# An attention-then-soft-MoE kernel: V's beacons loaded into a tile of their own, slot inputs with x as the stationary operand, and a reordered output group

## The chip, the cores and the metric

The kernel runs on one core of a Trainium2 chip. The core has a matrix engine (TensorE, PE in the profile, whose weight loads are listed as PEld), a vector engine (VectorE, DVE), a scalar engine (ScalarE, ACT), a general engine (GpSimd, POOL) and a sync engine (SP), and its transfers run on 16 DMA engines. In this kernel SP issues the loads of q, k, v and the beacons and the stores of the output (queue q1 of the profile), and POOL issues the loads of the expert weights, which are turned from float32 into float16 on the way (queue q0). The metric is the device time of one execution in microseconds (us); lower is better. The profile comes from one execution, and the times from several.

## The reference

Attention with 16 beacon keys and values ahead of the 576 causal ones, per batch and head, and behind it a soft mixture of experts over all 4608 tokens:

```python
B, H, S, Nb, D = 8, 8, 576, 16, 64
k_all = concat([beacon_k, k], axis=2); v_all = concat([beacon_v, v], axis=2)
scores = q @ k_all.T / sqrt(D)           # causal mask on the 576 keys, none on the beacons
a = softmax(scores); attn = a @ v_all
x = attn.transpose(0, 2, 1, 3).reshape(4608, 512)
logits = x @ phi                         # 32 slots: 8 experts of 4
slot_input = softmax(logits, axis=0).T @ x
slot_out[e] = relu(slot_input[e] @ w1[e]) @ w2[e]     # w1 512x1024, w2 1024x512
out = softmax(logits, axis=1) @ slot_out
```

## The kernel before

The order of all instructions is written out by hand. The main loop runs over 32 pairs of heads (`n`, four to a batch), and `lists[n]` names the pieces of work of one pass in order: `S0` to `S3` are the four score steps (PE into PSUM, then an exponential on ACT into the tile `ex`, then causal masks by POOL on the steps 1 to 3; `M` is the mask of step 0, on DVE). `A0` and `A1` multiply the previous pair's `ex` by V and, after `A1`, DVE normalises into `xb` (L434 and L435). `Qa`, `Qb`, `Ka` and `Kb` transpose q and k of later pairs on PE and copy them out on DVE (L377). `X0`, `X12` and `X34` transpose x, `L0` and `L1` make the logits of a half batch, `D` transposes the exponentials into `dT`, and `SI` adds one batch to the slot inputs.

V reaches the core as float32 in the tiles `vr` (two loads per batch, 128 partitions, two rows of V per partition, three buffers) and `vl` (the last rows), and POOL converts it into the float16 tile `vh` of the batch: pieces `c0`, `c1` (`cast_r`, L441, one 128x1024 instruction each) and `e0`, `e1` (`cast_vl`, L457, two 48x256 instructions each). `d0` and `d1` (`dup`, L451, DVE) copy a part of `vh` into `vd`. The first of the two `vr` loads of a batch (L145) brings 128 partitions, of which the first 8 are the place of the beacons; `load_bv` (L152) then loads the batch's beacons over these 8 partitions, so it waits until the first load has landed. `c0` converts both together. Loads are asked for one or two passes ahead through the table `asks`; SP issues them in that order, each when its buffer is free.

`SI` has two forms. For batches 0 to 5 it is `si_moving` (L564): `dT` is the stationary operand, 32 columns wide, and x moves, 512 columns at a time, in five matmuls; DVE adds the 128x512 result to `siq` (L568). `si_turn` (piece `SX`, L574, once, in pass 30) sums the four groups of rows of `siq` and turns them into `siacc` with eight float32 matmuls against the constant `slc`. For batches 6 and 7 it is `si_piece` (L551): x is the stationary operand (a 128x128 weight load for each of 20 matmuls) and `dT` moves, 32 columns, and DVE adds a 128x128 result (L556).

The expert weights come in 37 tiles of 2048 float16 columns. `want(n)` sets how many POOL has issued by pass `n`; the last ones (`wx`) go into the buffers of q and k that have become free and are loaded in halves. The very last six (L209) hold the left halves (`hf` 0) and then the right halves (`hf` 1) of the last three tiles of w2. POOL clears `hTz` (L696) ahead of the last seven issues.

After the loop come the last logits, layer 1 (L764), `turn` (L781) and layer 2 (L794) of the experts. `slot_out(0)` ends the left 256 columns of the slot outputs `soh` and `slot_out(1)` the right ones, which need the last weights. `group(cg, o, w)` makes the output of 512 tokens for `w` columns from column `o`: four matmuls (L838), each read out of PSUM by ACT (L840) or DVE (L843) in turn, and a store for every two. The order is: groups 0 and 1 left, `slot_out(1)`, group 2 left, groups 0 to 2 right, then groups 3 to 8 whole.

Of the kernel before, what the change touches and what calls it, by code (L numbers as in the profile page):

```python
# [8 lines left out]
FP = mybir.dt.float32  # L9
F16 = mybir.dt.float16  # L10
BF = mybir.dt.bfloat16
AL = mybir.AluOpType
# [5 lines left out]
def kernel(  # L18
# [21 lines left out]
    NCH = 5  # L40
    UL = U - 4 * P
    UE = (UL + Nb) // 2
    J = S // 64
    NP = B * H // 2
    NDC = Dm // P
# [31 lines left out]
    POS = [0, 2, 1, 3, 4]  # L77
# [50 lines left out]
    vr, vl = {}, {}  # L128
    vrows = v.rearrange("b h s d -> (b h s) d")

    def load_r(b, r):
# [15 lines left out]
        else:  # L147
            nc.sync.dma_start(out=t[:, :, :], in_=v[b, :, 2 * P - Nb:4 * P - Nb, :].rearrange(
                "h (p t) d -> p h (t d)", t=2))

    def load_bv(b):
        nc.sync.dma_start(out=vr[(b, 0)][0:Nb // 2],  # L152
                          in_=beacon_v[b].rearrange("h (p t) d -> p h (t d)", t=2))


    bv0 = exq.tile([P, H, 2 * D], FP, name="bv0", tag="ex")
# [72 lines left out]
    def dcols(x, c):  # L229
        o = 2 * P * (c // 2) + c % 2  # L230
        return x[:, o:o + 2 * P - 1:2]
# [70 lines left out]
    siT = const.tile([P, NDC, NSL], F16, name="siT")  # L302


    siq = const.tile([P, Dm], FP, name="siq")
    slc = const.tile([P, NSL], FP, name="slc")
# [8 lines left out]
    scs = [ps_sc.tile([P, 2, 512], FP, name=f"sc{i}") for i in range(2)]  # L315

    def late_constants():
        nc.vector.memset(siq[:, :], 0.0)
        nc.gpsimd.memset(slc[:, :], 0.0)
        for c in range(P // NSL):  # L320
            nc.gpsimd.affine_select(out=slc[:, :], in_=slc[:, :], compare_op=AL.not_equal, fill=1.0,
                                    base=-NSL * c, pattern=[[-1, NSL]], channel_multiplier=1)
        nc.gpsimd.memset(ssel[:, :, :], 0.0)
        for gr in range(E // EG):
            for i in range(EG):
                nc.gpsimd.affine_select(
                    out=ssel[:, gr, i * SPE:(i + 1) * SPE], in_=ssel[:, gr, i * SPE:(i + 1) * SPE],
                    compare_op=AL.not_equal, fill=1.0,
                    base=-(NSL * i + (gr * EG + i) * SPE), pattern=[[-1, SPE]], channel_multiplier=1)
# [115 lines left out]
    def cast_bv0():  # L445
        nc.vector.tensor_copy(
            out=vh[0][0:Nb // 2, 0:2, :, 0:D].rearrange("p s h d -> p h s d"),
            in_=bv0[0:Nb // 2].rearrange("p h (s d) -> p h s d", s=2))

    def dup(b, r):  # L450
        nc.vector.tensor_copy(out=vd[b % 2][64 * r:64 * r + 64, :, r, :, :],  # L451
                              in_=vh[b % 2][0:64, 2 * r:2 * r + 2, :, :])

    def cast_vl(b, r):
        t = vl[b]
        for i in range(2):
# [103 lines left out]
    def si_moving(b):  # L560
        sp = ps_tr.tile([P, Dm], FP, name="tr", tag="tr")
        for i in range(NCH):
            m, c = P if i < 4 else UL, i % 4
            nc.tensor.matmul(  # L564
                sp[NSL * c:NSL * c + NSL, :], dT[b][0:m, i, :],
                xb[b % 2][0:m, POS[i], :, :].rearrange("p h d -> p (h d)"),
                start=i < 4, stop=i in (1, 2, 3, 4))
        nc.vector.scalar_tensor_tensor(out=siq[:, :], in0=sp[:, :], scalar=2.0 ** -8,  # L568
                                       in1=siq[:, :], op0=AL.mult, op1=AL.add)

    def si_turn():
        sp = ps_tr.tile([P, NDC, NSL], FP, name="tr", tag="tr")
        for t in range(NDC):
            nc.tensor.matmul(sp[:, t, :], dcols(siq, t), slc[:, :],  # L574
                             start=True, stop=True)
        nc.vector.tensor_copy(out=siacc[:, :, :], in_=sp[:, :, :])

    order = ["S1 A0 L1 M S2 Qa Qb S3 A1 Ka S0", "S1 D A0 SI M S2 Kb S3 A1 X0 c0 S0",
             "S1 A0 M S2 Qa Qb S3 A1 X12 d0 c1 S0", "S1 A0 L0 M S2 e0 Ka Kb S3 A1 X34 d1 e1 S0"]
    lists = {n: order[n % 4].split() for n in range(NP)}


    lists[0] = "S2 M bv S3 S0 c1 d0 d1 e0 e1".split()
    lists[1] = "S1 S2 S3 M T2 A0 A1 S0".split()
    lists[2] = "S1 A0 M BC S2 T3 A1 S3 S0 BT c0".split()  # L590
    lists[3] = "S1 A0 M S2 T4 e0 A1 S3 e1 T5 c1 S0".split()
    lists[4] = "S1 A0 M d0 S2 Qa Qb S3 A1 d1 Ka S0".split()
    lists[5] = "S1 A0 M S2 Kb S3 A1 X0 c0 S0".split()
    lists[NP - 5] = "S1 A0 L0 M S2 Ka Kb S3 A1 X34 e0 S0".split()
    lists[NP - 4] = "S1 A0 L1 M S2 Ta Tb S3 e1 A1 d1 S0".split()
    lists[NP - 3] = "S1 D A0 SI M S2 Ta Tb S3 A1 X0 S0".split()
    lists[NP - 2] = "S1 A0 X12 M S2 X34 A1 L0 S3 SX S0".split()
    lists[NP - 1] = "S1 A0 P0 M S2 P1 A1 L1 S3 D".split()
    routing = {"X0": lambda b: xt_piece(b, (0,)), "X12": lambda b: xt_piece(b, (1, 2)),
               "X34": lambda b: xt_piece(b, (3, 4)), "L0": lambda b: logit_piece(b, 0),  # L600
               "L1": lambda b: logit_piece(b, 1), "D": lambda b: dt_piece(b),
               "SI": lambda b: (si_moving if b < B - 2 else si_piece)(b)}


    def idle_work(t, m):
# [3 lines left out]
    def do(n, w):  # L609
        b, g = divmod(n, H // 2)  # L610
        if w in routing:
            rb = b - 1
            if w == "SI" or n < NP - 1 and w in ("L1", "D"):
                rb = b - 2
            if rb >= 0:
                routing[w](rb)
        elif w in ("Qa", "Qb", "Ka", "Kb"):
            transp4(n // 2 + 1, "QK".index(w[0]), "ab".index(w[1]))
        elif w[0] == "T":
            m, ws = (n + 2, ("ab".index(w[1]),)) if w[1] in "ab" else (int(w[1]), (0, 1))  # L620
            for x in ws:
                transp(m, x)
        elif w == "BC":
            beacon_cast(1, B)
        elif w == "BT":
            beacon_t(1, B)
        elif w == "M":
            mask_f(n)
        elif w == "SX":
            si_turn()  # L630
        elif w[0] == "P":
            xt_pair(int(w[1]))
        elif w[0] == "A":
            if n >= 1:
                attend(n - 1, int(w[1]))
        elif w == "S0":
            if n + 1 < NP:
                score(n + 1, 0)
        elif w[0] == "S":
            score(n, int(w[1]))  # L640
        elif w == "bv":
            cast_bv0()
        elif w[0] in "cde":

            vb = 0 if n < 2 else b if g == 0 else b + 1
            if vb >= B:
                pass
            elif w[0] == "e":
                cast_vl(vb, int(w[1]))
            elif w[0] == "c":  # L650
# [33 lines left out]
    for n in range(NP):  # L684
        b, g = divmod(n, H // 2)
        if n + 2 < NP and n not in (2, 3):
            beacon_k_in(n + 2, nc.gpsimd)
        for w in lists[n]:
            if n == 3 and w == "M":
                beacon_k_in(n + 1, nc.gpsimd)  # L690
                beacon_k_in(n + 2, nc.gpsimd)
            if n == 6 and w == "M":
                for r in range(4):
                    nc.vector.tensor_copy(out=phih[:, :, r, :], in_=phif[:, :, :])
            if n == NP - 1 and w == "D":
                nc.gpsimd.memset(hTz, 0.0)  # L696
            if w == ("e0" if n == 3 else "D" if n == NP - 1 else "S0"):
                while wl < want(n):
                    load_w(wl)
                    wl += 1  # L700
            do(n, w)
        for what, vb in asks.get((n, 0), []):
            what(vb)
        for m in (5, 6) if n == 0 else (n + 6,):
            if m < NP:
                load_pair(m)
        for what, vb in asks.get((n, 1), []):
            what(vb)
# [119 lines left out]
    sc_scope.close()  # L828
    ps_f = ctx.enter_context(tc.tile_pool(name="ps_f", bufs=4, space=PSUM, side="right"))

    def group(cg, o, w):
        dst = out[cg * P * G:(cg + 1) * P * G, :].rearrange("(p j) d -> p j d", j=G)
        for j0 in range(0, G, 2):
# [58 lines left out]
```

## Time and profile before

| | us |
|---|---|
| median of 3 runs | 196.21 (194.69, 196.21, 201.97) |
| the profiled execution's own time | 195.3 |
| its span, first to last instruction | 193.6 |
| busy in the span: PE / DVE / ACT / POOL | 156.8 / 146.6 / 129.5 / 119.1 |
| period of the loop per batch (xb at 57.73, 75.00 and 92.25) | 17.27 and 17.25 |
| last weight issue at, landing after | 158.4, 10.3 |
| issue of output stores, from and to | 166.5, 187.8 |

Times inside the profile count from the start of the span. A row such as "POOL ex L387 <- ACT ex L403: 32.8, 49, 1.9" reads: the instruction at line 387 on POOL waited in total 32.8 us, 49 times, at most 1.9, for line 403 on ACT. Rates of transfers count the bytes that are written: a weight that is read as float32 and written as float16 counts half of what is read from memory. In the tables of stretches each engine has its busy time with the number of instructions; the last three columns are the granted TensorE clock, the busy share of the 16 DMA engines (packets of two queues may overlap, so it can be over 1) and GB/s.

### The profile page before, as it was taken

Reading aid. Unit: us, or ns where it says so; the run is one execution under the profiler, and the core shown is the slowest. Engines: PE = TensorE matmul, PEld = TensorE weight load, DVE = VectorE, ACT = ScalarE, POOL = GpSimd, SP = SyncE. Lnnn points to the kernel's source line nnn. Section 1 sums busy time; section 2 is a strip of 40 time slices with the busy share of each in tenths; the row PEclk is TensorE's granted clock in tenths of the full one; section 3 lists DMA queues with packets and bytes.
Section 4 is the critical chain, followed back from the end, with each engine's and each line's share of the span. In section 5 each row is a group of like instructions: output and inputs, shape, how many; then the busy total and the mean of one; then the engine's idle time right before and its main releaser. Section 6 shows DMA issues by size and latency. Waiting matters only on the chain.

```text
span 193.6 us, 7169 instructions
## 1 busy us (share of the span) xinstructions
PE 156.8 (81%) x2985; PEld 110.3 (57%) x2985; DVE 146.6 (76%) x306; ACT 129.5 (67%) x190; POOL 119.1 (62%) x278
## 2 busy tenths in 40 slices
PE   2569996989998989999998999999889999688300
PEld 1327674666676756767665766677567867343000
DVE  3595999989898988889898987997776524599500
ACT  3474876878788878879877877888668131399400
POOL 7996597678478858856875888697756860000000
PEclk9999999999999999999999999999999999999855
DMA  5999999999999999999999999999999999999995
GB/s 182 324 334 367 374 349 294 290 325 242 282 275 346 285 260 314 312 305 263 370 287 271 299 295 311 259 261 225 215 216 212 210 203 197 198 362 407 419 420 232
DMA packets 45048, 56.11 MB, mean 290 GB/s; under 512 B 4191, under 2 KB 30295, under 8 KB 45015
## 3 DMA queue, kind: packets, MB, share of 16 engines
q1 hardware_dynamic: 36359, 38.87, 58.7%
q0 software_dynamic: 8656, 16.78, 46.5%
q8 instruction: 23, 0.38, 0.7%
q14 instruction: 10, 0.08, 0.1%
HBM read 62.98 MB, written 9.44 MB: 374 GB/s over the span
## 4 chain that ended last, share of the span: by engine, by line
DVE 48%; PE 26%; issue 6%; DMA 5%; POOL 4%; ACT 3%; DVEq 0%; POOLq 0%; ACTq 0%
DVE xb L435 12%; PE av L426 9%; DVE qT L377 9%; DVE kT L377 8%; DMA wx<-in_moe_w_dram 5%; PE sc L396 4%; PE tr L375 4%; PE tr L486 4%; DVE ex L413 3%; DVE osb L843 3%; DVE kT L362 2%; DVE siq L568 2%; DVE qT L362 2%; ACT ex L403 2%; PE tr L564 2%
## 5 line engine op out<-in xcount | busy, mean ns | idle before, releaser
L403 ACT ACTIVATE ex<-sc 128x928 f16<-128x928 f32 (+2 forms) x128 | 106.4, 868 | 28.0 <-PE sc L396 20.6
L387 POOL TENSOR_SCALAR_AFFINE_SELECT ex<-ex 128x256 f16<-128x256 f16 x128 | 51.3, 414 | 35.4 <-ACT ex L403 32.8
L426 PEld LDWEIGHTS <-ex 128*128 128x128 f16 (+1 forms) x960 | 42.2, 106 | 18.2 <-issue 17.5
L396 PE MATMUL sc<-qT,kT 64*64 64x128 bf16 (+3 forms) x640 | 46.1, 264 | 4.8 <-DVE kT L382 2.2
L426 PE MATMUL av<-vh,ex 128*128 128x65 f16 x819 | 42.1, 199 | 0.1
L396 PEld LDWEIGHTS <-kT 64*64 64x64 bf16 (+1 forms) x640 | 17.6, 104 | 20.9 <-issue 7.9
L426 PE MATMUL av<-vd,ex 128*128 128x130 f16 x126 | 21.9, 225 | 8.7 <-DVE xb L435 6.6
L435 DVE TENSOR_TENSOR xb<-av,r 128x640 f16<-128x640 f32 (+1 forms) x32 | 26.0, 814 | 1.1
L377 DVE COPY kT<-tr 128x640 bf16<-128x640 bf16 (+1 forms) x24 | 18.0, 772 | 4.0 <-PE tr L375 4.0
L377 DVE COPY qT<-tr 128x640 bf16<-128x640 bf16 (+1 forms) x24 | 17.5, 769 | 3.2 <-PE tr L375 3.2
L413 DVE TENSOR_TENSOR ex<-ex,fmask 128x672 f16<-128x672 f16 x32 | 19.1, 595 | 0.4 <-ACT ex L403 0.2
L840 ACT ACTIVATE osb<-fp,rc 128x256 f32<-128x256 f32 (+1 forms) x24 | 12.9, 579 | 7.3 <-PE fp L838 6.7
L441 POOL CAST vh<-vr 128x1024 f16<-128x1024 f32 x15 | 16.0, 1066 | 0.1
L843 DVE TENSOR_SCALAR osb<-fp,rc 128x256 f32<-128x256 f32 (+1 forms) x24 | 13.7, 614 | 0.7 <-PE fp L838 0.6
L457 POOL CAST vh<-vl 48x256 f16<-48x256 f32 x32 | 13.2, 413 | 1.3
L838 PE MATMUL fp<-soh,eLh 128*128 128x256 f16 (+1 forms) x48 | 11.4, 325 | 2.6 <-ACT osb L840 1.5
L476 DVE COPY xT<-tr 128x512 f16<-128x512 f16 (+1 forms) x21 | 10.6, 504 | 0.9 <-PE tr L471 0.9
L471 PE MATMUL tr<-idh,xb 128*128 128x128 f16 (+1 forms) x140 | 10.8, 215 | 0.4 <-DVE qT L377 0.4
L375 PE MATMUL tr<-idb,kf 128*64 128x128 bf16 x216 | 9.9, 224 | 0.8 <-DVE qT L377 0.8
L838 PEld LDWEIGHTS <-eLh 128*128 128x128 f16 x48 | 5.3, 114 | 8.3 <-issue 6.5
L486 PE MATMUL tr<-xT,phih 128*128 128x288 f16 x56 | 9.2, 286 | 0.0
L375 PEld LDWEIGHTS <-kf 128*64 128x64 bf16 x216 | 7.1, 109 | 3.5 <-issue 3.3
(122 smaller groups left out, 199.3 us busy)
## 6 DMA issues: line engine op xcount, KB each, us to landing
w<-in_moe_w_dram POOLq DMA_DIRECT2D x27, 512.0 KB, 8.8
qf<-in_q_dram SPq DMA_DIRECT2D x32, 288.0 KB, 7.4
kf<-in_k_dram SPq DMA_DIRECT2D x32, 288.0 KB, 6.2
vr<-in_v_dram SPq DMA_DIRECT2D x15, 512.0 KB, 6.6
out_dram<-osb SPq DMA_DIRECT2D x12, 512.0 KB, 5.7
out_dram<-osb SPq DMA_DIRECT2D x11, 256.0 KB, 3.0
wx<-in_moe_w_dram POOLq DMA_DIRECT2D x10, 256.0 KB, 9.8
vl<-in_v_dram SPq DMA_DIRECT2D x16, 96.0 KB, 10.2
```

The lines of the kernel that those rows point to most:

```text
L375: nc.tensor.transpose(tp[64 * r:64 * r + 64, j - j0, :], ts[r][:, j, :].bitcast(BF)[:, 1::2], idb[:, :])
L377: nc.vector.tensor_copy(out=dst[:, :, Nb:Nb + S].rearrange("p a (s j) -> p a s j", j=J)[:, :, :, j0:j1], in_=tp[:, :, :].rearrange("p j (a ...
L387: nc.gpsimd.affine_select(out=x, in_=x, compare_op=AL.is_ge, fill=0.0, base=base, pattern=pattern, channel_multiplier=cm)
L396: nc.tensor.matmul(sc[p0:p0 + kn, a, col:col + un], kT[n // 2 % 2][64 * a:64 * a + 64, n % 2, k0:k0 + ks * (kn - 1) + 1:ks], qT[n // 2 % 2 ...
L403: nc.scalar.activation(x[:, :, o:o + w], sc[:, :, 0:w], AF.Exp, scale=scale)
L413: nc.vector.tensor_tensor(out=x, in0=x, in1=fmask[:, :].unsqueeze(1).broadcast_to([P, 2, XT + UL]), op=AL.min)
L426: nc.tensor.matmul(dst, ex[n][0:kn, a, o:o + m], rhs, start=j in first, stop=j in final)
L435: nc.vector.tensor_tensor(out=xb[b % 2][:, :, h0:h0 + dh * (na - 1) + 1:dh, :].rearrange("p i a d -> p a i d"), in0=avv[:, :, :, 0:D], in1 ...
L441: eng.tensor_copy(out=vh[b % 2][:, 2 * r:2 * r + 2, :, 0:D].rearrange("p s h d -> p h s d"), in_=vr.pop((b, r))[:, :, :].rearrange("p h (s ...
L486: nc.tensor.matmul(lp[:, 0:w], phih[:, t, :, :].rearrange("p r e -> p (r e)"), xT[b][:, t, Nb + hf * w:Nb + (hf + 1) * w], start=(t == 0), ...
L838: nc.tensor.matmul(fp_[:, 0:w], etok(cg, j), soh[:, o:o + w], start=True, stop=True)
L843: nc.vector.tensor_scalar(out=osb[:, j - j0, o:o + w], in0=fp_[:, 0:w], scalar1=rc[:, i:i + 1], scalar2=None, op0=AL.mult)
```

## The change

V's beacons of the batches 1 to 7 get a tile `bv` of their own (one buffer, 64 partitions, the heads in two halves), loaded by two DMAs, and two POOL instructions per batch convert them into the first 8 partitions of `vh` after `c0` has written there (pieces `b0` and `b1`). For the last batch the load is asked for half a pass later. `siq`, `slc`, `si_moving` and `si_turn` go; every batch uses `si_piece`, and `siacc` is cleared by POOL at the start. In the lists of passes 2 to 5 some of the pieces `c0`, `d0`, `d1`, `e0` and `e1` move. `hTz` is cleared as float32, with half as many elements. `slot_out(1)` moves from ahead of group 2 left to between its two halves.

```diff
     def load_bv(b):
-        nc.sync.dma_start(out=vr[(b, 0)][0:Nb // 2],
-                          in_=beacon_v[b].rearrange("h (p t) d -> p h (t d)", t=2))
+        bvs[b] = vlp.tile([64, H // 2, 2 * D], FP, name="bv", tag="bv")
+        for r in range(2):
+            nc.sync.dma_start(
+                out=bvs[b][32 * r:32 * r + Nb // 2],
+                in_=beacon_v[b, H // 2 * r:H // 2 * (r + 1)].rearrange(
+                    "h (p t) d -> p h (t d)", t=2))
...
     def late_constants():
-        nc.vector.memset(siq[:, :], 0.0)
-        nc.gpsimd.memset(slc[:, :], 0.0)
-        for c in range(P // NSL):
-            nc.gpsimd.affine_select(out=slc[:, :], in_=slc[:, :], compare_op=AL.not_equal, fill=1.0,
-                                    base=-NSL * c, pattern=[[-1, NSL]], channel_multiplier=1)
+        nc.gpsimd.memset(siacc[:, :, :], 0.0)
...
+    def cast_bv(b, r):
+        nc.gpsimd.tensor_copy(
+            out=vh[b % 2][0:Nb // 2, 0:2, H // 2 * r:H // 2 * (r + 1), 0:D].rearrange(
+                "p s h d -> p h s d"),
+            in_=bvs[b][32 * r:32 * r + Nb // 2].rearrange("p h (s d) -> p h s d", s=2))
...
-    order = ["S1 A0 L1 M S2 Qa Qb S3 A1 Ka S0", "S1 D A0 SI M S2 Kb S3 A1 X0 c0 S0",
-             "S1 A0 M S2 Qa Qb S3 A1 X12 d0 c1 S0", "S1 A0 L0 M S2 e0 Ka Kb S3 A1 X34 d1 e1 S0"]
+    order = ["S1 A0 L1 M S2 Qa Qb S3 A1 Ka S0", "S1 D A0 SI M S2 Kb S3 A1 X0 c0 b0 S0",
+             "S1 A0 M S2 b1 Qa Qb S3 A1 X12 d0 c1 S0", "S1 A0 L0 M S2 e0 Ka Kb S3 A1 X34 d1 e1 S0"]
...
-    lists[2] = "S1 A0 M BC S2 T3 A1 S3 S0 BT c0".split()
-    lists[3] = "S1 A0 M S2 T4 e0 A1 S3 e1 T5 c1 S0".split()
-    lists[4] = "S1 A0 M d0 S2 Qa Qb S3 A1 d1 Ka S0".split()
-    lists[5] = "S1 A0 M S2 Kb S3 A1 X0 c0 S0".split()
+    lists[2] = "S1 A0 M BC S2 c0 T3 A1 S3 S0 BT".split()
+    lists[3] = "S1 A0 M S2 b0 T4 A1 S3 e0 T5 c1 S0".split()
+    lists[4] = "S1 A0 M S2 b1 Qa Qb S3 A1 d0 d1 e1 Ka S0".split()
+    lists[5] = "S1 A0 M S2 Kb S3 A1 X0 c0 b0 S0".split()
...
-    lists[NP - 2] = "S1 A0 X12 M S2 X34 A1 L0 S3 SX S0".split()
+    lists[NP - 2] = "S1 A0 X12 M S2 X34 A1 L0 S3 S0".split()
...
-               "SI": lambda b: (si_moving if b < B - 2 else si_piece)(b)}
+               "SI": lambda b: si_piece(b)}
...
-        for key, what in (((n0, 0), lambda x: load_r(x, 0)), ((n1, 1), load_bv),
+        for key, what in (((n0, 0), lambda x: load_r(x, 0)),
+                          ((NP - 9, 0) if vb == B - 1 else (n1, 1), load_bv),
...
-                nc.gpsimd.memset(hTz, 0.0)
+                nc.gpsimd.memset(hTz.bitcast(FP), 0.0)
...
-    def group(cg, o, w):
+    def group(cg, o, w, js=range(0, G, 2)):
...
     for cg in range(NL):
+        group(cg, 0, HD, (0,))
         if cg == NL - 1:
             slot_out(1)
-        group(cg, 0, HD)
+        group(cg, 0, HD, (2,))
```

More of the change, by code (lines that the diff above doesn't have):

```diff
@@ L149, in load_r @@
                 "h (p t) d -> p h (t d)", t=2))
+    bvs = {}
     def load_bv(b):
-        nc.sync.dma_start(out=vr[(b, 0)][0:Nb // 2],
-                          in_=beacon_v[b].rearrange("h (p t) d -> p h (t d)", t=2))
+        bvs[b] = vlp.tile([64, H // 2, 2 * D], FP, name="bv", tag="bv")
[4 more added lines that the diff above has]
+                    "h (p t) d -> p h (t d)", t=2))
     bv0 = exq.tile([P, H, 2 * D], FP, name="bv0", tag="ex")
@@ L302 @@
     siT = const.tile([P, NDC, NSL], F16, name="siT")
-    siq = const.tile([P, Dm], FP, name="siq")
-    slc = const.tile([P, NSL], FP, name="slc")
     ssel = const.tile([P, E // EG, EG * SPE], F16, name="ssel")
@@ L558, in si_piece @@
             scalar=2.0 ** -8, in1=siacc[:, :, :], op0=AL.mult, op1=AL.add)
[L560 to L576, printed above, removed]
-    order = ["S1 A0 L1 M S2 Qa Qb S3 A1 Ka S0", "S1 D A0 SI M S2 Kb S3 A1 X0 c0 S0",
-             "S1 A0 M S2 Qa Qb S3 A1 X12 d0 c1 S0", "S1 A0 L0 M S2 e0 Ka Kb S3 A1 X34 d1 e1 S0"]
+    order = ["S1 A0 L1 M S2 Qa Qb S3 A1 Ka S0", "S1 D A0 SI M S2 Kb S3 A1 X0 c0 b0 S0",
+             "S1 A0 M S2 b1 Qa Qb S3 A1 X12 d0 c1 S0", "S1 A0 L0 M S2 e0 Ka Kb S3 A1 X34 d1 e1 S0"]
     lists = {n: order[n % 4].split() for n in range(NP)}
@@ L628, in do @@
             mask_f(n)
-        elif w == "SX":
-            si_turn()
         elif w[0] == "P":
@@ L642, in do @@
             cast_bv0()
-        elif w[0] in "cde":
+        elif w[0] in "bcde":
             vb = 0 if n < 2 else b if g == 0 else b + 1
@@ L649, in do @@
                 cast_vl(vb, int(w[1]))
+            elif w[0] == "b":
+                cast_bv(vb, int(w[1]))
             elif w[0] == "c":
@@ L829 @@
     ps_f = ctx.enter_context(tc.tile_pool(name="ps_f", bufs=4, space=PSUM, side="right"))
-    def group(cg, o, w):
+    def group(cg, o, w, js=range(0, G, 2)):
         dst = out[cg * P * G:(cg + 1) * P * G, :].rearrange("(p j) d -> p j d", j=G)
-        for j0 in range(0, G, 2):
+        for j0 in js:
             osb = wh.tile([P, 2, Dm], FP, name="osb", tag="w")
```

## The prediction

> **What bounds the kernel now.** The page first, for the transfers:
>
> ```profile
> GB/s 182 324 334 367 374 349 294 290 325 242 282 275 346 285 260 314 312 305 263 370 287 271 299 295 311 259 261 225 215 216 212 210 203 197 198 362 407 419 420 232
> HBM read 62.98 MB, written 9.44 MB: 374 GB/s over the span
> ```
>
> The rate is counted on the written side, and the weights (16.78 MB written by q0) are read as twice as much. So the 215 GB/s of the slices from about 131 to 165 us, where only weights are under way, are some 430 GB/s of reading, the 420 at the end are plain stores, and the whole is 72.4 MB in 193.6 us. The table of stretches:
>
> ```profile
> core 0: us, PE busy (x) PEld busy (x) DVE busy (x) ACT busy (x) POOL busy (x), PEclk, DMA share, GB/s
> 75.00:92.25 17.25, 15.96 (x314) 11.40 (x318) 15.00 (x30) 14.11 (x20) 12.54 (x30) 1.00 1.08 305
> ...
> 130.00:150.00 20.00, 18.02 (x359) 13.30 (x357) 15.14 (x34) 14.98 (x24) 13.52 (x32) 1.00 1.08 218
> ...
> 166.00:168.00 2.00, 1.41 (x18) 0.73 (x17) 1.75 (x4) 1.66 (x4) 0.00 (x0) 1.00 0.73 149
> 168.00:171.00 3.00, 1.86 (x13) 1.13 (x13) 1.79 (x5) 1.72 (x4) 0.00 (x0) 1.00 0.89 306
> 171.00:176.00 5.00, 4.24 (x19) 1.96 (x18) 4.91 (x9) 4.80 (x10) 0.00 (x0) 1.00 1.09 382
> 176.00:191.00 15.00, 4.21 (x15) 1.42 (x13) 5.67 (x9) 4.76 (x8) 0.00 (x0) 0.72 1.03 420
> ```
>
> The DMA engines are busy all through; the one hole is 166 to 171. In a batch of the loop (second row) three weight tiles add 1.57 MB of reading that is not counted: 305 is really 305 + 1570/17.25 = 396 GB/s. So the loop is paced by the engines, with the transfers close behind; from 130 on the transfers have a queue (the last weight takes 10.3 us to land) and set the end. Next the chain of waits:
>
> ```profile
> 51.27 0.62 PE tr L564 x5
> 51.91 0.69 DVE siq L568
> ...
> 145.21 1.07 PE tr L574 x8
> ...
> 158.40 10.28 DMA wx<-in_moe_w_dram
> ...
> 169.65 0.94 ACT osb L840 x2
> ```
>
> The slot inputs stand on the chain in the loop and at 145, but the chain then goes through the last weight (158.40 + 10.28 = 168.7). The last evacuation ends at 181, ten us before the last store lands. The left half of the last weights lands at 155.04 + 9.5 = 164.5, and PE uses it from 164.42 on: engines and transfers reach that point together. Being earlier there on the engines' side gains nothing, since the weights cannot come sooner out of a full queue; being later pushes the stores.
>
> **The change, part by part.**
>
> Beacons on SP's queue. Removed is this wait, 6.3 us in six places:
>
> ```profile
> SPq L152 <- DMA vr<-in_v_dram: 6.3, 6, 2.4
> ```
>
> Behind it on SP stand a `vr` load and the next pairs' q and k. Nobody waits for those: the only wait of PE for q is 3.8 us at the start. So 0; for the same reason the second beacon issue (0.29 us, seven times) costs 0 while q and k arrive early. Bound: if that cover were gone, 0.29 per batch, 2.0 in all.
>
> The two conversions on POOL. No row has 8x512. By free size it lies between 48x256 (0.40 us) and 128x1024 (1.07); in between, 0.63. Per batch:
>
> ```profile
> 55.84 1.31 POOL L387 TENSOR_SCALAR_AFFINE_SELECT ex<-ex 128x256 f16<-128x256 f16 x3
> 57.67 0.41 POOL L387 TENSOR_SCALAR_AFFINE_SELECT ex<-ex 128x256 f16<-128x256 f16 x1 [0.52 <-ACT ex L403]
> 58.03 1.06 POOL L441 CAST vh<-vr 128x1024 f16<-128x1024 f32 x1
> ...
> 58.60 0.22 PE L426 MATMUL av<-vd,ex 128*128 128x130 f16 x1 [0.32 <-DVE xb L435]
> ```
>
> (The first three are POOL's timeline, the last PE's.) `b0` goes ahead of the three masks, `b1` ahead of the fourth. That mask is needed by the A0 at 58.60, by its third product. POOL was idle 0.52 before it and it was ready 0.52 early, so it delays A0 by 2 x 0.63 - 1.04 = 0.22 per batch, six batches: +1.3. Bounds: 0 (at 0.40) and 6 x (2.14 - 1.04) = +6.6. Behind it `c1` runs 0.74 later, beside DVE's `vd` copy at 59.07: that row takes 0.41, but 1.28 at 29.21 beside a cast (28.96 to 30.21). The extra 0.87 falls into DVE's idle 0.70 before 60.60 and the 0.22 by which PE is late anyway: 0.
>
> A rule speaks here: the Trainium skill, SBUF — State Buffer, SBUF: two separate sides, says that VectorE in a two-port mode and GpSimd lock their shared port for a whole instruction and the other fully blocks. The row at 29.21 agrees; by the rule alone every such meeting would cost up to a whole cast, an estimate of 6 x 1.07 = 6.4 us over the loop before any cover.
>
> Slot inputs with x stationary. DVE: 0.69 becomes 0.28 (row L556), six times. PE: five matmuls (0.61) against
>
> ```profile
> 152.37 0.66 PE L551 MATMUL tr<-dT,xb 128*128 128x32 f16 x20
> 152.88 0.41 PE L512 MATMUL sc<-vh,phih 128*128 128x288 f16 x2
> ```
>
> twenty in 0.66, with the next step 0.51 after their start: equal. Of DVE's 0.41 little arrives: PE goes on without a gap from the slot input to A1's end at 53.48 and the reciprocal starts at 53.56, so at most 0.08 a batch, and I take 0.04: -0.2 (bounds 0 and -2.5). `si_turn` goes from PE's path: -1.1 at 145.
>
> The same skill's page TensorE: Matmul & The Clock Gate, Back-to-back issue gap, has pairs of weight load and matmul at 81 ns each; twenty would be an estimated 1.6 us, 1.1 more per batch. The row's 0.51/20 = 26 ns says otherwise here, and decides.
>
> At the start POOL loses 1.06 + 0.12 for `slc` and gains a memset of some 0.2; DVE loses 0.48 (`siq`). The masks and casts of the first pair follow: between 0 and -1.0, I take -0.5. The moved pieces of passes 2 to 5 are the same instructions; the one `vd` copy of 1.28 may shrink or another may grow, ±0.9, taken as 0.
>
> On the engines' side this is +1.3 - 0.2 - 1.1 - 0.5 = -0.5 at 164.4: no delay, and no gain, because the weights land at 164.5.
>
> `hTz`: 1.83 becomes about 1.08 (row 128x1040 float32) ahead of seven weight issues. 0: their landings follow each other at 0.6 to 1.5 us out of the queue, and the last issue even waits for a landing.
>
> Group 2 left. Two tiles (0.47 on ACT, 0.48 on DVE) move into the wait for the last weight: ACT is idle 1.6 us before 169.28, DVE 1.26 before 169.06. PE's two matmuls come before sixteen that end at 168.99, of which the last four wait for 168.7. So 256 KB of stores start while the engines of the hole have room: 0.26 MB / 382 GB/s = 0.69, or one evacuation of 0.48 less later; I take -0.6. The whole hole holds 2 x (382 - 149) + 3 x (382 - 306) = 0.69 MB, 1.8 us, the most that could be filled; the least is 0.
>
> **Sum.** 195.3 - 0.6 = 194.7 in the profiled execution's terms. The median shown is 0.9 above that execution, and scaled to it the sum is 195.6; with one of its three runs at 201.97 I take 195.0. About 2% is what a measurement of this kernel can tell from no change: 192.3 and 200.1 around the median.
>
> **Rivals.**
>
> *Nothing arrives* (0.14): the two tiles' stores only take the room of the last weight pieces, since these share the DMA engines. 195.3. For: at 166 to 168 weights are still landing. Against: the share there is 0.73.
>
> *The engines set the end* (0.13): if weights would come earlier with an earlier loop, every cut counts: -2.5 (`siq`), -1.1, -1.0, -0.75 (`hTz`), -0.6: 195.3 - 5.95 = 189.3. For: DVE has 48% of the chain and `siq` is on it. Against: 396 of some 425 GB/s are in use in the loop already, and the queue from 130 on.
>
> *POOL becomes late* (0.17): at 1.07 a cast, as the 128x1024 row has, A0 waits 1.1 us a batch, +6.6 - 0.2 - 1.1 - 0.5 = +4.8 at 164.4. Then the weights are all there, the DMA engines stand idle until the first store, and the reordered group hides nothing: 195.3 + 4.7 = 200.0. It starts to cost where 6 x (2c - 1.04) passes the 1.8 gained elsewhere, at 0.67 us a cast, and passes 2% (+4.0) from about 1.0. A beacon that lands late would do the same, as `b0` waits for it with all masks behind. For: four masks, three casts and a weight issue stand in one line there. Against: the row of 48x256, and POOL's 35.4 us of idle time before masks.
>
> *Weight loads of the slot inputs show* (0.04): if the 96 ns loads of L551 did not hide, 20 x 0.096 = 1.9 instead of 0.54 a batch, +8.3 - 0.5: some 203. The skill's 81 ns would give +6.0 by the same sum, an estimate. Against both: the row of L551.
>
> **How the numbers follow.** My forecast has 0.52, with its own range of 193.4 (hole filled whole, 193.5) to 196.2. Within 2%: 0.52 + 0.14 = 0.66. Faster: 0.13. Slower: 0.17 + 0.04 = 0.21. The range leaves out the engines' case and the weight loads (0.17) and takes in POOL's: 193.0 to 200.0.
>
> **What would show it.** Right: period per batch within 0.3 of 17.25; `b0` and `b1` near 0.6 us; no PE or POOL wait for beacons; last weight landing within 1 us of 168.7; the rate at 168 to 171 nearer 382; ACT at work before that landing. Wrong: a period over 18, A0 waiting for POOL masks (more than 0.3 each), or a weight landing several us earlier, which would mean that the queue was not full.

## The result: slower, and two passes of the loop that became long

The changed kernel takes 208.58 us (median of six runs, 203.5 to 209.21) against 196.28 for the kernel before (six runs, 194.69 to 201.97). The ratio is 1.044, 95% interval 1.0328 to 1.0553. The profiled execution took 203.5 us with a span of 201.8 (before: 195.3 and 193.6). The prediction was 195.0, range 193.0 to 200.0. Some runs of every kernel lie a few per cent above its others: ratios leave them out, medians do not.

The page of the changed kernel, for the transfers (granted clock and rate in 40 slices, then the queues):

```profile
PEclk9999998899999999999589999996999999999955
...
GB/s 194 281 309 353 347 296 296 288 312 293 250 282 308 264 276 309 296 238 304 322 287 277 269 327 269 250 266 228 216 214 210 207 184 194 141 316 374 408 407 263
...
q1 hardware_dynamic: 36415, 38.87, 60.5%
q0 software_dynamic: 8656, 16.78, 44.3%
...
HBM read 62.98 MB, written 9.44 MB: 359 GB/s over the span
```

The line of q1 on the page of the kernel before:

```profile
q1 hardware_dynamic: 36359, 38.87, 58.7%
```

The same 38.87 MB on q1 now takes each DMA engine 60.5% of 201.8 = 122.1 us in place of 58.7% of 193.6 = 113.6. The output stores at the end, which wait for nothing but themselves, run at 407 to 408 GB/s in place of 419 to 420. So the packets have become slower, also those of tiles that the change does not mention.

The table of stretches (us; busy PE, PEld, DVE, ACT, POOL; granted clock, DMA share, GB/s):

```profile
core 0: us, PE busy (x) PEld busy (x) DVE busy (x) ACT busy (x) POOL busy (x), PEclk, DMA share, GB/s
57.78:74.95 17.17, 15.98 (x329) 11.92 (x333) 15.28 (x30) 14.10 (x20) 13.10 (x31) 1.00 1.09 281
92.70:101.82 9.12, 6.34 (x77) 4.26 (x78) 3.94 (x7) 3.87 (x6) 7.31 (x16) 0.64 1.09 321
106.27:123.44 17.17, 15.99 (x331) 11.93 (x333) 15.29 (x31) 14.10 (x20) 13.56 (x31) 1.00 1.08 287
131.68:139.03 7.35, 5.32 (x78) 3.79 (x78) 3.94 (x8) 3.77 (x6) 6.09 (x13) 0.81 1.11 252
```

The same two passes in the kernel before:

```profile
92.25:96.72 4.47, 4.14 (x84) 3.06 (x88) 3.73 (x7) 3.74 (x6) 3.79 (x9) 1.00 1.09 369
126.75:131.22 4.47, 4.14 (x84) 3.06 (x88) 3.99 (x7) 3.74 (x6) 3.61 (x9) 1.00 1.11 257
```

A batch that nothing disturbs takes 17.17 us, a little less than before (17.25). The loss stands in two passes from one `xb` to the next that took 4.47 each before: 92.70 to 101.82 (9.12, so 4.65 more) and 131.68 to 139.03 (7.35, 2.88 more). Together that is 7.5 of the 8.2 us by which the span grew. In both the granted clock falls, to 0.64 and 0.81.

The chain of waits through the first of them (start, us, what):

```profile
61.33 11.91 DMA bv<-in_beacon_v_dram
...
79.60 13.16 DMA bv<-in_beacon_v_dram
92.80 0.08 issue
92.88 0.06 POOL vh L450
...
94.76 0.62 POOL vh L450
95.38 0.06 issue
95.44 1.08 POOL ex L386
96.53 0.05 issue
96.57 0.79 PE av L425 x10
```

The beacons were asked for at 79.60 and landed 13.16 us later; `b0` starts when they are there, the masks stand behind it on POOL, and the fourth mask holds PE up until 96.57. Twice in this trace the chain runs through such a load. The waits on SP's queue fit:

```profile
SPq L107 <- PE sc L395: 14.3, 16, 4.6
SPq L107 <- DMA vr<-in_v_dram: 14.2, 9, 3.3
```

The same rows of the kernel before:

```profile
SPq L107 <- PE sc L396: 35.2, 18, 5.0
SPq L107 <- DMA vr<-in_v_dram: 3.9, 4, 1.6
```

Before, SP (at L107, the loads of q and k) waited 35.2 us for PE to free a buffer, and 3.9 us for a load of V to land; now it waits 14.3 and 14.2. The loads, which had been ahead, are what is late.

The second long pass has no late load in it. POOL's timeline, then DVE's, then PE's:

```profile
129.52 0.76 POOL L450 CAST vh<-bv 8x512 f16<-8x512 f32 x1
130.23 1.43 POOL L214 DMA_DIRECT2D w<-in_moe_w_dram  x2
131.66 0.22 POOL L381 COPY kT<-bkT 128x16 bf16<-128x16 bf16 x1
131.80 1.12 POOL L386 TENSOR_SCALAR_AFFINE_SELECT ex<-ex 128x256 f16<-128x256 f16 x3
132.99 0.61 POOL L450 CAST vh<-bv 8x512 f16<-8x512 f32 x1
133.67 1.07 POOL L386 TENSOR_SCALAR_AFFINE_SELECT ex<-ex 128x256 f16<-128x256 f16 x1
...
133.63 0.42 DVE L456 COPY vd<-vh 64x1040 f16<-64x1040 f16 x1 [0.53 <-POOL vh L450]
133.98 0.49 DVE L412 TENSOR_TENSOR ex<-ex,fmask 128x672 f16<-128x672 f16 x1
...
134.80 0.52 PE L425 MATMUL av<-vh,ex 128*128 128x65 f16 x10 [1.61 <-POOL ex L386]
```

POOL is busy without a gap: `b0`, two weight issues (1.43), three masks, `b1`, the fourth mask. PE waits 1.61 us for that mask. And the mask, 0.41 elsewhere, takes 1.07: DVE's `vd` copy, which `b1` has just released, and its mask of step 0 run beside it.

### The profile page after: what moved, and what is told of

Its sections match the earlier page's. It is cut to its first block, busy times and chain, and to the rows that moved or that the text cites. A ratio compares the mean times of both kernels' runs of the same rounds, so it can differ in the third digit from the quotient of the medians.

```text
span 201.8 us, 7357 instructions
## 1 busy us (share of the span) xinstructions
PE 160.5 (80%) x3067; PEld 114.8 (57%) x3067; DVE 144.7 (72%) x304; ACT 129.0 (64%) x190; POOL 126.2 (63%) x288
## 3 DMA queue, kind: packets, MB, share of 16 engines
q1 hardware_dynamic: 36415, 38.87, 60.5%
## 4 chain that ended last, share of the span: by engine, by line
PE 36%; DVE 23%; DMA 17%; POOL 8%; issue 5%; ACT 3%; DVEq 0%; SPq 0%; POOLq 0%; ACTq 0%
DMA bv<-in_beacon_v_dram 12%; PE av L425 10%; PE sc L395 6%; DVE xb L434 6%; DMA kf<-in_k_dram 4%; DVE qT L376 4%; POOL ex L386 4%; PE tr L374 4%; PE tr L491 3%; DVE kT L376 3%; DVE osb L831 2%; PE tr L556 2%; DVE kT L361 2%; PE tr L359 2%; POOL vh L450 2%
## 5 line engine op out<-in xcount | busy, mean ns | idle before, releaser
L386 POOL TENSOR_SCALAR_AFFINE_SELECT ex<-ex 128x256 f16<-128x256 f16 x128 | 53.1, 430 | 30.1 <-ACT ex L402 26.8
L425 PEld LDWEIGHTS <-ex 128*128 128x128 f16 (+1 forms) x960 | 43.5, 108 | 24.4 <-issue 18.6
L395 PE MATMUL sc<-qT,kT 64*64 64x128 bf16 (+3 forms) x640 | 46.9, 267 | 5.3 <-ACT ex L402 2.3
L425 PE MATMUL av<-vh,ex 128*128 128x65 f16 x819 | 44.1, 201 | 4.5 <-POOL ex L386 4.3
L425 PE MATMUL av<-vd,ex 128*128 128x130 f16 x126 | 22.4, 228 | 9.4 <-DVE xb L434 5.8
L495 ACT ACTIVATE eLh<-tr 128x288 f16<-128x288 f32 x14 | 5.8, 412 | 10.3 <-PE tr L491 10.3
L476 PE MATMUL tr<-idh,xb 128*128 128x128 f16 (+1 forms) x140 | 11.7, 226 | 0.0
L450 POOL CAST vh<-bv 8x512 f16<-8x512 f32 x14 | 9.0, 644 | 3.7 <-DMA bv<-in_beacon_v_dram 3.0
L456 DVE COPY vd<-vh 64x1040 f16<-64x1040 f16 x16 | 8.9, 555 | 3.0 <-POOL vh L450 2.8
L374 PE MATMUL tr<-idb,kf 128*64 128x128 bf16 x216 | 10.9, 241 | 0.0
(115 smaller groups left out, 201.8 us busy)
```

The lines of the kernel that those rows point to most:

```text
L374: nc.tensor.transpose(tp[64 * r:64 * r + 64, j - j0, :], ts[r][:, j, :].bitcast(BF)[:, 1::2], idb[:, :])
L386: nc.gpsimd.affine_select(out=x, in_=x, compare_op=AL.is_ge, fill=0.0, base=base, pattern=pattern, channel_multiplier=cm)
L395: nc.tensor.matmul(sc[p0:p0 + kn, a, col:col + un], kT[n // 2 % 2][64 * a:64 * a + 64, n % 2, k0:k0 + ks * (kn - 1) + 1:ks], qT[n // 2 % 2 ...
L425: nc.tensor.matmul(dst, ex[n][0:kn, a, o:o + m], rhs, start=j in first, stop=j in final)
L450: nc.gpsimd.tensor_copy(out=vh[b % 2][0:Nb // 2, 0:2, H // 2 * r:H // 2 * (r + 1), 0:D].rearrange("p s h d -> p h s d"), in_=bvs[b][32 * r ...
```

## The experiments

All ratios are to the kernel before on the same chip. "Aligned" is explained at e5.

| run | what it is | median us | ratio, 95% interval |
|---|---|---|---|
| e1 | all but the beacons' tile | 206.23 | 1.0347 (1.0233, 1.0461) |
| e2 | changed, beacons asked earlier | 209.2 | 1.052 (1.0366, 1.0673) |
| e3 | e1, beacon load in two | 203.05 | 1.0349 (1.024, 1.0457) |
| e4 | e1, two POOL casts more | 210.17 | 1.0491 (1.0339, 1.0644) |
| e5 | changed, aligned | 200.29 | 1.020 (1.0099, 1.0301) |
| e6 | before, shifted by 128 bytes | 203.99 | 1.0305 (1.0204, 1.0406) |
| e7 | e1, aligned | 195.47 | 0.9967 (0.9915, 1.0019) |
| e8 | changed, only weights and output aligned | 205.85 | 1.0489 (1.0395, 1.0583) |
| e9 | e7, beacon load in two | 203.23 | none: four runs, 195.37 to 206.34 |
| e10 | e7, two POOL casts more | 199.31 | 1.0198 (1.0125, 1.0272) |
| e11 | e5, beacons asked earlier | 205.13 | 1.0341 (1.0229, 1.0453) |
| e12 | the tail alone | 195.45 | 0.9997 (0.9959, 1.0036) |
| e13 | e7, all tiles 1024 bytes further | 196.25 | 1.0026 (0.998, 1.0073) |
| e14 | e10 without its shift | 199.4 | 1.0242 (1.0137, 1.0347) |
| e15 | e5 with 13 loads per batch | 197.48 | 1.0043 (0.9988, 1.0098) |
| e16 | before, shifted by 64 bytes | 205.51 | 1.0493 (1.0396, 1.0589) |
| e17 | e5 again | 201.48 | none: six runs, 196.82 to 203.26 |
| e18 | e9 again | 197.81 | 1.0074 (1.0025, 1.0123) |

### First theories: the beacons, and the parts one by one (e1 to e4)

The first theory was that the beacons' own load, now late on SP's queue, is the cause; its rivals were POOL's conversions and the new slot inputs. e1 has the slot inputs, the tail and `hTz` of the change, and the beacons as before:

> The kernel before with every part of the change except the beacons' own tile (x stationary for every batch, hTz cleared as float32, group 2 left around slot_out(1); lists 2 to 5 as before). Theory L (the beacon transfers land late, POOL waits for them with the masks behind, PE waits for the masks): 194 to 196 us, period per batch 17.2, no pass over 5.5 us after pass 6. Rival S (the time of the two conversions on POOL): the same here. Rival P (the slot inputs or the reordered tail cost the time): 200 or more.

It measured 1.0347: most of the loss with no part of the beacons' change in it. In its profiled run (210.53 us, the longest of four) PE waits 11.2 us for one q load that took 19.8 us from issue to landing.

e2 asks for the beacons one pair of heads earlier:

```diff
-                          ((NP - 9, 0) if vb == B - 1 else (n1, 1), load_bv),
+                          ((n0, 1), load_bv),
```

> The kernel after, with one line changed: the beacons of a batch are asked for one pair of q and k earlier on SP's queue. Theory L: the beacons land two or more us ahead of b0, the waits of POOL for them go, and the time falls to 195 to 199. Rival S: it stays at 203 to 209, as the conversions are all still there. Rival W (SP's window of eight transfers in flight, which has 14 transfers a batch to pass instead of 13, makes q, k and V late too): the beacons are in time, but SP's waits for landed transfers stay at 14 us or more and POOL then waits for V or PE for q and k: 199 to 205.

1.052: no help. e3 and e4 put one cost each on top of e1, a second SP transfer for the beacons and two POOL conversions that nobody reads:

```diff
-        nc.sync.dma_start(out=vr[(b, 0)][0:Nb // 2],
-                          in_=beacon_v[b].rearrange("h (p t) d -> p h (t d)", t=2))
+        for r in range(2):
+            nc.sync.dma_start(out=vr[(b, 0)][0:Nb // 2, H // 2 * r:H // 2 * (r + 1)],
+                              in_=beacon_v[b, H // 2 * r:H // 2 * (r + 1)].rearrange(
+                                  "h (p t) d -> p h (t d)", t=2))
```

> e1_rest with its beacon load (into V's tile) split into two transfers of four heads each, so that SP passes 14 transfers a batch, with nothing added on POOL. Rival W: 3 to 8 us slower than e1_rest, with SP's waits on landed transfers up. Theory L without W, and rival S: within 1.5 us of e1_rest.

```diff
+    dmy = const.tile([Nb // 2, 512], F16, name="dmy")
...
-    order = ["S1 A0 L1 M S2 Qa Qb S3 A1 Ka S0", "S1 D A0 SI M S2 Kb S3 A1 X0 c0 S0",
-             "S1 A0 M S2 Qa Qb S3 A1 X12 d0 c1 S0", "S1 A0 L0 M S2 e0 Ka Kb S3 A1 X34 d1 e1 S0"]
+    order = ["S1 A0 L1 M S2 Qa Qb S3 A1 Ka S0", "S1 D A0 SI M S2 Kb S3 A1 X0 c0 b0 S0",
+             "S1 A0 M S2 b1 Qa Qb S3 A1 X12 d0 c1 S0", "S1 A0 L0 M S2 e0 Ka Kb S3 A1 X34 d1 e1 S0"]
...
+        elif w in ("b0", "b1"):
+            if n >= 5:
+                nc.gpsimd.tensor_copy(
+                    out=dmy[0:Nb // 2, :].rearrange("p (r x) -> p r x", r=4),
+                    in_=phif[0:Nb // 2, :, :].rearrange("p c e -> p (c e)").unsqueeze(1).broadcast_to(
+                        [Nb // 2, 4, P]))
```

> e1_rest with two more conversions of 8x512 on POOL in each of six batches, at the places of b0 and b1, from a constant into a scratch tile that nobody reads (no transfer to wait for). Rival S: most of the 8 us is here, 200 or more. Theory L: at most 1.3 us over e1_rest (0.22 a batch).

1.0349 and 1.0491 against e1's 1.0347, with overlapping intervals. Neither the beacons' load, nor a second transfer, nor the conversions can explain e1, which has none of them. The time fits the last rival, the slot inputs or the tail; e7 below excludes it. What e1 shares with the changed kernel, and what no theory had looked at, is that two tiles are gone.

### Where the tiles lie (e5 to e8, e16)

`siq` is 2048 bytes per partition and `slc` 128. Without them every later tile lies 2176 bytes lower (behind `bv`, which takes 2048 bytes, 128 lower). Both are 128 bytes off a multiple of 256: `qf`, `kf`, `vr`, the weights `w` and the output `osb` start on multiples of 256 bytes before, and 128 past one in the changed kernel. The mean duration of the packets in the traces, ns:

| queue, packet | before | changed | e5 | e6 | e7 | e8 | e16 |
|---|---|---|---|---|---|---|---|
| q1, 512 B (V) | 28.1 | 31.7 | 28.7 | 31.6 | 28.2 | 31.6 | 31.7 |
| q1, 2304 B (q, k) | 100.5 | 106.3 | 100.3 | 105.9 | 100.1 | 105.9 | 106.7 |
| q1, 1024 B (output) | 46.4 | 48.8 | 46.5 | 49.0 | 46.5 | 46.3 | 47.9 |
| q0, 4096 B (weights) | 327.7 | 323.7 | 328.4 | 330.9 | 325.3 | 331.3 | 325.0 |

There are 19960, 8192 and 3072 of the first three kinds: 19960 x 3.6 + 8192 x 5.8 + 3072 x 2.4 ns = 127 us, over 16 engines 7.9 us each; with 1536 packets of 4096 bytes (159.2 before, 163.5 changed) it is 8.3, nearly all of the 8.5 that the profile's line of q1 grew by.

The Trainium skill's page DMA: Bandwidth & Descriptors, section How a descriptor splits into AXI transactions, says that a descriptor that does not start on a 256-byte address begins with a piece from the boundary below, so that a size that is a multiple of 256 bytes needs one piece more: three for two at 512 bytes, ten for nine at 2304. The Trainium skill tells this of what is read. The trace agrees as far as it goes: it shows no pieces, but 3.6 ns more for 512 bytes and 5.8 more for 2304, in loads whose tile is the side that is written.

An unused tile puts the addresses back, or, in the kernel before, moves them:

```diff
     siT = const.tile([P, NDC, NSL], F16, name="siT")
+    pad = const.tile([P, NSL], FP, name="pad")
```

> The kernel after plus an unused tile of 128 bytes a partition where the constant slc was, and nothing else. Taking out siq and slc moved every tile that a transfer writes or reads (qf, kf, vr, vl, wh) from a multiple of 256 bytes to 128 past one; the tile moves them back. Theory A (transfers into and out of tiles that do not start on 256 bytes are slower, and the loop's loads have no room for it): 193 to 197 us, mean 512-byte packet of q1 back from 32 to 28 ns, 2304-byte from 106 to 100, no pass over 5.5 us after pass 6. Theory L (beacons late through SP's order): 200 or more, as order and transfers are unchanged.

> The kernel before plus the same unused tile of 128 bytes, which moves its tiles to 128 past a multiple of 256. Theory A: 200 to 208 us, packets of q1 slower as in after, passes of 6 us and more in the loop. Theory L and every theory that blames an instruction: as before, 195 to 197.

> e1_rest (all parts of the change but the beacons' own tile) with the same tile of 128 bytes. Theory A: 193 to 196.5 us, against 202 to 210 without it. If the slot inputs with x stationary cost the time themselves: 200 or more.

e7 is the clearest: the same 128 unused bytes take e1 from 1.0347 to 0.9967, and from 45 us on the passes are all of their normal length again. e6 is its mirror: the kernel before, with nothing but an unused tile, goes to 1.0305. e5 takes the changed kernel from 1.044 to 1.020, its median to 200.29; the 193 to 197 expected are not reached, and the next section is about the rest. e8 puts the unused tile behind the loads' tiles, so only weights and output lie well:

```diff
+    pad = sml.tile([P, 32], FP, name="pad", tag="pad", bufs=1)
     NW = 24
```

> The kernel after with the 128 bytes put ahead of the weight tiles only, so that weights and output tiles start on 256 bytes again and q, k, V and beacons do not. Theory A with the loads to blame: still 199 to 208, with the loop's long passes; only the output's 1024- and 4096-byte packets go back to 46 and 159 ns, and the last 25 us gain under 1 us. If it is the weights or the output: 194 to 197.

1.0489: the output packets are quick again, and nothing is gained. It is the loads ahead of them, of q, k, V and the beacons, that matter. e16 shifts the kernel before by 64 bytes:

```diff
+    pad = const.tile([P, 16], FP, name="pad")
```

> The kernel before with an unused tile of 64 bytes in place of 128 (e6). If it is the crossing of 256-byte boundaries that costs, 64 bytes cost as much as 128: packets of 512 bytes on q1 about 31.6 ns against 28.1, of 2304 about 106 against 100.5, and 1.02 to 1.04 of before. If the cost grows with the offset, or sits at 128: packets nearer 30 and 103, 1.005 to 1.02.

1.0493, above the expected 1.02 to 1.04, and the packets as at 128. So for a packet being off the boundary costs, and 64 bytes as much as 128; why the whole time is longer than e6's is not shown.

e16 also shows what the slower packets do without any other change to the kernel. From issue to landing its loads of q, k and V take 8.3, 7.2 and 7.4 us (medians), in place of 7.4, 6.2 and 6.6 before and 7.0, 6.2 and 6.3 in e7. At 112.34 POOL has waited 3.07 us for a beacon load, and the pass from 112.54 takes 7.69 us. Its undisturbed batches take 17.23 to 17.25 us, as before, so it is not the instructions that have become slower.

### What is left of the loss when the tiles lie well (e9 to e15, e17, e18)

e5 is still 2% slow. Four kernels take e7 and e5 apart further: e9 is e7 with e3's edit, e10 with e4's, e11 is e5 with e2's, and e12 is the kernel before with the reordered group 2 and the new clear of `hTz` alone.

> The kernel e7 (slot inputs, tail, no beacon tile, tiles on 256-byte addresses again: 0.997 of before) with the beacon load split in two, so that SP has 14 transfers per batch as in the changed kernel, and nothing more for POOL. What is asked: why the changed kernel on aligned addresses (e5) still took 1.020 of before. If the 14th transfer on SP's queue, of which eight can be under way, is the cause: 1.015 to 1.025, a late load of q or v in the trace. If it is the two conversions on POOL, or the time at which the beacons are asked for: 0.99 to 1.005.

> The same e7 with two 8x512 conversions more per batch on POOL, in the places of b0 and b1, into a tile that nobody reads, from data that is always there; the loads are those of before, 13 per batch, on 256-byte addresses. If POOL's time for the conversions is the cause of the rest in e5 (0.61 each beside 1.04 of cover, six batches): 1.015 to 1.025. As the prediction had it (0.22 a batch, all covered by the weights' landing): 0.995 to 1.005.

> The changed kernel with the 128-byte unused tile (e5) and the beacons of every batch asked for one pair of heads earlier, so also for the last batch, where e5 showed POOL waiting 3.65 us for them. If the rest of e5 is the late ask of the beacons: 0.99 to 1.005, no POOL wait for bv above 1 us. If it is the 14th transfer or POOL's time: as e5, 1.01 to 1.03.

> The kernel before with the reordered output group (and the quicker clear of hTz) alone; no tile moves. The prediction's one gain: -0.6 us, 0.997 of before (bounds 1.0 and 0.991). If its rival 'nothing arrives' holds: 1.000.

e11 excludes the late ask: asking earlier does not help (1.0341, its interval overlaps e5's). e12, the tail alone, gains nothing (0.9997). e10 has POOL's conversions alone at 1.0198; but its `dmy` also moved the tiles by 1024 bytes, and part of its loss came before the first added conversion ran. e9's runs lie too far apart. So e13 (the tile `dmy` without the conversions), e14 (the conversions, with `dmy` behind the loads' tiles) and e15, which takes the 14th transfer out of e5 and so leaves out the beacons of half the heads:

```diff
-        for r in range(2):
+        for r in range(1):
             nc.sync.dma_start(
                 out=bvs[b][32 * r:32 * r + Nb // 2],
...
-            in_=bvs[b][32 * r:32 * r + Nb // 2].rearrange("p h (s d) -> p h s d", s=2))
+            in_=bvs[b][0:Nb // 2].rearrange("p h (s d) -> p h s d", s=2))
```

> The kernel e7 with the unused 1024-byte tile of e10 and without its conversions: all later tiles lie 1024 bytes further, still at multiples of 256. In e10's trace the time was lost between 26 and 40 us, before the first of the added conversions ran. If the place of the tiles by more than 256 bytes matters: 1.015 to 1.025 as e10. If only the offset within 256 bytes matters: 0.99 to 1.005.

> e10 with the unused tile behind the loads' tiles, so that q, k and v lie exactly where they lie in e7, and the two conversions per batch on POOL as in e10. If the conversions make the loss: 1.015 to 1.025. If it was the place of the tiles, or if the conversions are covered as the prediction had it: 0.99 to 1.005.

> The changed kernel on 256-byte addresses (e5) with one beacon load per batch in place of two: the second half of the heads' beacons is left out, and both conversions read the first half. 13 transfers on SP's queue per batch, as before, with both conversions. If the 14th transfer makes the rest of e5: 0.99 to 1.005. If POOL's conversions or the tile of the beacons make it: 1.01 to 1.03.

e13: 1.0026, so a shift by 1024 bytes costs nothing that shows. e14: 1.0242, so the conversions alone do make a loss. Its timelines of POOL, PE and DVE say where:

```profile
127.60 1.43 POOL L208 DMA_DIRECT2D w<-in_moe_w_dram  x2
129.03 0.22 POOL L378 COPY kT<-bkT 128x16 bf16<-128x16 bf16 x1
129.17 1.12 POOL L383 TENSOR_SCALAR_AFFINE_SELECT ex<-ex 128x256 f16<-128x256 f16 x3
130.24 0.60 POOL L617 CAST dmy<-phif 8x512 f16<-8x512 f32 x1
130.80 0.40 POOL L383 TENSOR_SCALAR_AFFINE_SELECT ex<-ex 128x256 f16<-128x256 f16 x1
...
131.25 0.52 PE L422 MATMUL av<-vh,ex 128*128 128x65 f16 x10 [0.70 <-POOL ex L383]
...
130.40 2.08 DVE L447 COPY vd<-vh 64x1040 f16<-64x1040 f16 x1
132.41 0.48 DVE L409 TENSOR_TENSOR ex<-ex,fmask 128x672 f16<-128x672 f16 x1
133.00 1.46 DVE L373 COPY kT<-tr 128x640 bf16<-128x640 bf16 x2
```

The same place of e7, without conversions:

```profile
124.04 1.44 POOL L207 DMA_DIRECT2D w<-in_moe_w_dram  x2
125.47 0.22 POOL L377 COPY kT<-bkT 128x16 bf16<-128x16 bf16 x1
125.62 1.48 POOL L382 TENSOR_SCALAR_AFFINE_SELECT ex<-ex 128x256 f16<-128x256 f16 x4
```

In the last batch's pass two weight issues stand on POOL ahead of the masks, and there is no idle time left. With the conversions PE waits 0.70 and the pass takes 5.54 us in e14 and 5.57 in e10, in place of 4.47 in e7. DVE is late there by nearly as much: its `vd` copy takes 2.08 beside POOL's work (0.70 at the same place of e7), and its mask ends at 132.89, only 0.11 before the copy to `kT` that PE's wait holds up. So the 1.07 cannot be put down to the mask alone. In the batches between 47.70 and the last one the conversions cost nothing: from 47.70 to 125.12 e14 needs 77.42, and e7 77.45 for the same passes. The rest of e14's loss is once at the start (35.86 to 47.70, 11.84 against 9.01), where DVE's four casts of phi take 2.53 in place of 1.32 beside POOL's casts and PE's clock then falls to 0.86.

e5 and e9 were run again, more often, as e17 and e18:

> e5 once more, with more runs. The traces of e13 and e15 show that one pass near 122 us, in which PE waits 5 to 7 us for a q load, comes in some runs of a kernel and not in others; e5's profiled run had it, and four runs are too few to tell its share. If the change on 256-byte addresses is slower in itself: 1.01 to 1.03 again, hardly a run under 197.5. If e5's 1.020 came from this one late load alone: part of the runs at 195 to 197.5, and 1.00 to 1.01.

> e9 once more, with more runs: the slot inputs, the tail and 14 transfers per batch, without POOL's conversions. If the 14th transfer makes the late load more frequent: more than half of the runs above 198.5, where e7 (13 transfers) had one of ten and e15 (13) four of ten. If not, less than a third above 198.5.

e17 has no ratio: its six runs are 196.82, 198.71 and four from 201.33 to 203.26, beside a median of 196.47 and a lowest run of 194.37 of the kernel before; one lies under 197.5, where hardly one was expected. That e5's loss was not one late load alone is shown by the profiled run (198.7 us): it has no late load in the loop, and its POOL and PE show the same place as the changed kernel:

```profile
129.16 1.07 POOL L387 TENSOR_SCALAR_AFFINE_SELECT ex<-ex 128x256 f16<-128x256 f16 x1
...
130.29 0.52 PE L426 MATMUL av<-vh,ex 128*128 128x65 f16 x10 [1.62 <-POOL ex L387]
```

That pass takes 7.33 us (127.17 to 134.50), 2.86 more than before, of a span that is 3.4 longer. So the pass is about 1.1 longer where nothing depends on the conversions (e14), and 2.9 where `b1` releases DVE's copy into the time of the fourth mask (the changed kernel, e17).

e18: 1.0074 for the 14th transfer without conversions, a small loss; 5 of 12 runs are above 198.5, between the two expectations, beside 4 of 17 of the kernel before. e15, with 13 loads and both conversions, is at 1.0043, on another chip, and its fastest run at 195.0. By e17's pass alone it should hardly come below 197 (the fastest run of before beside it, 194.3, and 2.9; e17's own fastest is 196.82). Its profiled run does not settle this: there a q load came late, PE waited 7.3 us for it, POOL worked off its queue meanwhile and was then idle for 6.32, and the pass that follows takes 4.50. Why e15 is so much nearer to before than e17 stays open.

No version beats the kernel before measurably; e7 comes nearest (0.9967, interval up to 1.0019).

## Why the prediction was wrong, point by point

**"Beacons on SP's queue", "So 0".** This is the step that failed first. The sum looked at who waits for the loads, and took their durations as given: every load's packets were costed at the durations of before. The two removed tiles were costed only as the memsets that fall away, and what lies behind them in memory was not asked. The runs show 3.6 to 5.8 ns more on each packet of q, k and V, 7.9 us more on each DMA engine, in a loop that the prediction itself had put at 396 of some 425 GB/s. The cover that was named ("while q and k arrive early") was there before and went: SP's wait for landed loads of V grew from 3.9 to 14.2 us. Its price with the cover gone, 2.0, was that of the second issue; measured, e1 costs 3.8% more than e7, some 7 us, and the changed kernel 1.044 in place of e5's 1.020. The rival *POOL becomes late* did name a beacon that lands late, with `b0` and all masks behind it, which is the first long pass; but it named no reason why it should.

**"It delays A0 by 0.22 per batch, six batches: +1.3."** The price of a conversion was right (0.63 taken; 0.61 mostly, 0.77 at worst). The step failed in taking one batch for all six. It used the idle 0.52 before the mask at 57.67. In four batches the cost is 0 (17.15 to 17.16 us a batch in e17, from 58.55 to 127.17); the first of the six lies in the start of the loop, where it cannot be told from the rest; in the last, where two weight issues stand ahead of the masks, the pass is 2.9 longer. The rival *POOL becomes late* had the right engine and the right mask, but saw it as 1.1 in each batch at a longer conversion, and set in only from 0.67 us a conversion as a mean.

**The rule on the shared port.** The prediction weighed the Trainium skill's page SBUF — State Buffer, section SBUF: two separate sides, on POOL's casts that hold up DVE. It put what stands behind `b1` at 0. The trace shows the other direction: the mask on POOL takes 1.07 in place of 0.41 beside DVE's copy and mask, wherever `b1` comes late and releases that copy just ahead of it (the changed kernel at 95.44 and 133.67, e17 at 129.16, e8 at 77.31, 115.51 and 135.93). In e14 nothing ties the copy to `b1`; it starts at 130.40 while POOL converts and takes 2.08, and the mask keeps its 0.40. So whoever comes first holds the other up, which is how the Trainium skill has it. It speaks of one instruction; the 2.08 reach over three of POOL's in a row, the conversion, the mask and `c1`.

**Slot inputs.** Right: twenty matmuls in 0.66, and a batch is 0.08 shorter (17.17 for 17.25), so -0.5 for the -0.2 taken. The 81 ns that the prediction took from the Trainium skill's page TensorE: Matmul & The Clock Gate, section Back-to-back issue gap, stand there for 128 moving columns; these matmuls move 32, so the price built on them had no ground. `si_turn` brought 0.37 (that pass took 5.39 and takes 5.02 in e7), not 1.1. Of the 0.5 at the start nothing is seen: the `xb` of 35.93 before comes at 35.95 in e7 and, with the moved pieces, at 36.59 in the changed kernel. None of it arrives, as forecast: in e7 the last `xb` is 0.9 earlier (151.95 for 152.87), the last weight lands at 157.06 + 11.32 = 168.4 for 168.7, and the span is 193.5 for 193.6.

**Group 2 left, -0.6.** e12 measures 0.9997 (0.9959 to 1.0036), span 193.7: the centre is on the rival *Nothing arrives*, though 0.997 lies inside the interval. The rate at 168 to 171 us rose, as forecast, from 306 to 340 GB/s, but at 166 to 168 it fell from 149 to 95; in that run the first store was issued at 166.98 in place of 166.48. Whether the reordering delays that store is not shown.

**"No PE or POOL wait for beacons."** Wrong: 2.40 at 92.88. **"Period within 0.3 of 17.25"** held in every undisturbed batch (17.17), which shows how little a period says about a kernel whose loss sits in two passes.

## What to carry to other kernels

When an edit removes or adds a tile, compare the addresses of all tiles that transfers write or read, before and after, and keep them on multiples of 256 bytes. A step that moves work onto an engine is priced in each pass in which it occurs, in the pass with the fullest queue first, not from one pass times their number. In this loop, near the limit of its transfers, 6 to 13% on the packets did not show as a longer period: they showed as a few long passes, the longest of the changed kernel 9.12 us in place of 4.47.

## What the runs showed that was not expected

- A start off a 256-byte address costs q1's packets 5.8 ns of 100.5 (2304 bytes) and 3.6 of 28.1 (512 bytes), at 64 bytes as at 128; by e13, tiles that lie 1024 bytes further cost nothing. The packets of q0, which convert on the way, show no change (327.7 and 323.7).
- 128 unused bytes per partition are worth 3.8% (e1 against e7).
- A wait of PE can cost more than its length: with the 1.62 us at 130.29 in e17 the pass is 2.86 longer and its granted clock 0.81; with the 0.70 in e14 the pass is 1.07 longer and the clock stays at 1.00.
